# Decay of the state, x's remainder and the parts of the next q and k issued behind the last step of P's parts

## The chip, the cores and the metric

One NeuronCore of a Trainium2 chip runs the whole program. The metric is the device time of one execution in microseconds (us). "Profiled execution" is one further execution, recorded instruction by instruction; every duration below comes from it.

## The reference

Two stages follow each other. The first is an mLSTM recurrence over 768 steps for 4 batches and 8 heads with heads of 40 numbers; its output, one row of 320 numbers for each of 3072 tokens, is the `x` of the second, a bilinear feed-forward block with 1536 hidden units. All inputs are float32.

```python
for t in range(S):                                   # batch b, head h
    m_new  = maximum(f_gate[t] + m, i_gate[t])
    f_stab = exp(f_gate[t] + m - m_new);  i_stab = exp(i_gate[t] - m_new);  m = m_new
    C = f_stab * C + i_stab * outer(v[t], k[t])
    n = f_stab * n + i_stab * k[t]
    y[t] = sigmoid(o_gate[t]) * (C @ q[t]) / maximum(abs(n . q[t]), 1)
...
out = ((x @ w_a) * (x @ w_b)) @ w_out                # x: 3072 x 320, d_ff 1536
```

## The kernel before

The recurrence is computed in chunks of 128 steps of one batch: 24 chunks, numbered `n`, four batches to a time step of 128. The feed-forward block (the code calls it `moe_block`) takes the tokens of 2 or 3 chunks at a time: nine blocks of 2, 2, 3, 3, 3, 3, 3, 2, 3 chunks, with 12 hidden tiles each (`up` makes a hidden tile, `down` adds its product with w_out). While TensorE works on block `k`, the chunks of block `k`+2 go through the recurrence; the chunks' pieces are dealt out between the block's matmuls by a ratio written in the main loop.

A chunk from number 6 on goes through these stages; chunks 0 to 5 take a shorter road (`begin_*`).

- `stage_a`: q and k are each split into three bfloat16 parts h, m and l. ScalarE (ACT) copies h (L508), VectorE (DVE) subtracts it, giving the remainder `r` (L512), ACT copies m from r (L513), and DVE, for chunks below 8 GpSimd (POOL), subtracts again to get l (L515). ACT lays the parts out once more (L518, L519), and SyncE's queue (SP) issues four DMA transposes into the tiles `T` (L522): two for q, two for k. `T` has one buffer for each of q and k.
- `stage_e`: the decay matrix `E`, tile `gbc`: a DMA from DRAM (L224, issued on SP), a mask on POOL (L483), and eight exponentials on ACT (L490). `gbc` has two buffers.
- `stage_b`, once for each half of the heads: TensorE (PE) makes the scores `pS` from `T` (L545), DVE multiplies them with E (L550), and the product P is split into three bfloat16 parts: ACT takes the first (L552), DVE subtracts it (L554), and a last DVE step makes the third (L556). The parts lie in `pb` and in the upper halves of `gbc`.
- `stage_i`: PE multiplies q's parts with the state (L571), DVE scales the result (L575).
- `stage_c`: PE multiplies P's parts with v's parts into `pV` (L603), the first four heads with the parts of half 0, the last four with those of half 1; DVE adds (L610).
- `stage_u`: PE makes the update of the state in `pU` (L628); DVE decays the state `cst` (L635) and adds the update (L639); ACT, POOL and DVE split the state, and DMAs bring the parts into place for the chunk four later (L646 to L659).
- `stage_f`: normaliser and output gate (L669 to L686). `stage_d`, for chunk n-1: PE transposes the output into `pX` (L707), ACT copies it into `xh` (L711), and DVE makes the remainder `xl` (L712). xh and xl are the feed-forward block's inputs.

`pS`, `pI`, `pX`, `pV` and `pU` take turns in two PSUM banks (tag `pat`), so each must wait until the one two places earlier has been read. The feed-forward products `pu` have three banks.

The order on each engine is not the order of the code: a scheduler, with a model of its own for the durations, orders all instructions of an engine by what is ready when. Each engine then runs its list strictly in order, and waits where the next entry is not ready. `tc.issue_after(x)` tells the scheduler that instructions traced in its block stand behind instruction `x` on that engine; it adds no wait on the chip, only a place in the list. In the code, the stages of a step come as B, D, E, A, C, U, F: chunk n's P, chunk n-1's x, chunk n+1's E and q/k parts, then chunk n's products, update and output.

Of the kernel before, what the change touches and what calls it, by code (L numbers as in the profile page):

```python
# [8 lines left out]
F32 = mybir.dt.float32  # L9
# [6 lines left out]
ALU = mybir.AluOpType  # L16
# [4 lines left out]
def kernel(  # L21
# [13 lines left out]
    nc = tc.nc  # L35
    B, H, S, D = q.shape
    DM, DFF = w_a.shape
    P = 128
# [3 lines left out]
    DV = D + 2  # L42
# [38 lines left out]
    HH = H // 2  # L81
# [10 lines left out]
    for j in range(3):  # L92
        r = slice(j * BH, (j + 1) * BH)
# [18 lines left out]
    dec = wpool.tile([P, NC - 2, BH // 2], F32, name="dec")  # L112
# [12 lines left out]
    after = {}  # L125
# [53 lines left out]
    def nat(n):  # L179
        return inner.get(n) or (qk[n % NQ], va[n % NQ])  # L180
# [146 lines left out]
    def beta_col(c, b):  # L327
        return g_col(c, b, 0)
# [35 lines left out]
    def need(x):  # L364

        while ready[0] < x:
            next(conv)
# [104 lines left out]
    def half(h):  # L472

        return h % 2 * 64, h % 2 * HH + h // 2, h // 2

    st = {}

    def stage_e(n):

        c, b = chunks[n]  # L480
        E = gbc.pop(n)
        st.setdefault(n, {})["E"] = E
        nc.gpsimd.affine_select(  # L483
            E, E, pattern=[[0, H], [1, P]], compare_op=ALU.is_ge, fill=-1e30, base=0,
            channel_multiplier=-1,
        )
        yield
        beta = beta_col(c, b)
        for h in range(H):
            nc.scalar.activation(E[:, h], E[:, h], AF.Exp, bias=beta[:, h:h + 1])  # L490
            if h % 2 == 1:
                yield

    def stage_a(n):

        c, b = chunks[n]
        s = st.setdefault(n, {})
        src = [x[..., 0:D] for x in nat(n)[0]]
        need(32)
        for _ in conv:  # L500
            pass

        at = {"h": (0, 2 * D), "m": (D, D), "l": (2 * D, 0)}
        s["T"] = []
        for j in range(2):
            qks = qks2[j]
            ph, pm, pl = (qks[:, 1, :, at[i][j]:at[i][j] + D] for i in "hml")
            nc.scalar.copy(ph, src[j])  # L508
            yield
            r = apool.tile([P, H * DV], F32, tag="tmp", name=f"r{n}_{j}")[:, 0:H * D]  # L510
            r = r.rearrange("t (h d) -> t h d", h=H)
            (nc.gpsimd if 2 * n + j < 4 else nc.vector).tensor_tensor(r, src[j], ph, op=ALU.subtract)  # L512
            nc.scalar.copy(pm, r)  # L513
            yield
            (nc.gpsimd if n < 8 else nc.vector).tensor_tensor(pl, r, pm, op=ALU.subtract)  # L515
            yield
            lo = (1 - j) * D
            nc.scalar.copy(qks[:, 0, :, lo:lo + 2 * D], qks[:, 1, :, D - lo:3 * D - lo])  # L518
            nc.scalar.copy(qks[:, 0, :, 2 * D * j:2 * D * j + D], ph)  # L519
            T = apool.tile([P, 2, H, P], BF16, tag=f"T{j}", name=f"T{n}_{j}", bufs=1)  # L520
            for w in range(2):
                nc.sync.dma_start_transpose(T[:, w], qks[:, w].rearrange("t h d -> t (h d)"))  # L522
            s["T"].append(T)
            yield
# [12 lines left out]
    def stage_b(n, hf):  # L537
        s = st[n]
        qT, kT = s["T"]
        pS = ps_at.tile([P, HH, P], F32, tag="pat", name=f"pS{n}_{hf}")  # L540
        K3 = 3 * D
        for x in range(HH):
            h = hf * HH + x
            for w in range(2):
                nc.tensor.matmul(  # L545
                    pS[:, x, :], kT[0:K3, w, h, :], qT[0:K3, w, h, :], start=(w == 0), stop=(w == 1)
                )
        yield
        E = s["E"][:, hf * HH:(hf + 1) * HH]
        nc.vector.tensor_tensor(E, pS, E, op=ALU.mult)  # L550
        pb = apool.tile([P, 2, HH, P], BF16, tag="pb", name=f"pb{n}_{hf}")
        nc.scalar.copy(pb[:, 0], E)  # L552
        yield
        nc.vector.tensor_tensor(E, E, pb[:, 0], op=ALU.subtract)  # L554
        mid = E.bitcast(BF16).rearrange("s h (t w) -> s h t w", w=2)[:, :, :, 1]
        nc.vector.tensor_tensor(pb[:, 1], E, mid, op=ALU.subtract)  # L556
        s[f"pb{hf}"] = (pb[:, 0], mid, pb[:, 1])
        yield

# [55 lines left out]
    def stage_u(n):  # L615
        c, b = chunks[n]
        if c == NC - 1:
            return
        vw = vws.pop(n)
        if NS <= n < 6:  # L620
            pU = ps_dn.tile([P, 512], F32, tag="pd2", name=f"pU{n}")
        else:
            pU = ps_at.tile([P, 512], F32, tag="pat", name=f"pU{n}")
        pu = pU[:, 0:HH * DV].rearrange("p (h d) -> p h d", h=HH)
        dense(n, pU, 3)
        for h in (*range(0, H, 2), *range(1, H, 2)):
            r, _, x = half(h)
            nc.tensor.matmul(  # L628
                pu[r:r + 64, x], nat(n)[0][1][:, h, :], vw[:, h], start=True, stop=True
            )  # L630
        t = cst[b]
        if c == 0:
            nc.scalar.copy(t, pu)
        else:
            nc.vector.tensor_tensor(  # L635
                t, t, dec[:, c - 1, b * HH:(b + 1) * HH].unsqueeze(2).broadcast_to([P, HH, DV]),
                op=ALU.mult,
            )
            nc.vector.tensor_tensor(t, pu, t, op=ALU.add)  # L639
        yield  # L640
        if n + B < NF32:
            return
        cb = apool.tile([P, 3, HH, DV], BF16, tag="cb", name=f"cb{n}", bufs=1)
        cr = apool.tile([P, H * DV], F32, tag="tmp", name=f"cr{n}")[:, 0:HH * DV]
        cr = cr.rearrange("t (h d) -> t h d", h=HH)
        nc.scalar.copy(cb[:, 2], t)  # L646
        nc.gpsimd.tensor_tensor(cr, t, cb[:, 2], op=ALU.subtract)
        yield
        if n < 8:
            nc.scalar.copy(cb[:, 1], cr)  # L650
        else:
            nc.vector.tensor_copy(cb[:, 1], cr)
        nc.gpsimd.tensor_tensor(cb[:, 0], cr, cb[:, 1], op=ALU.subtract)
        for j in range(2):
            cd = c_dram[b][:, :, j * HH:(j + 1) * HH].rearrange("i d h e -> d i h e")
            nc.sync.dma_start(cd[:, 3], cb[j * 64:j * 64 + D, 2])
            nc.sync.dma_start(cd[:, 0:3], cb[j * 64:j * 64 + D])
        for w in range(2):
            nc.sync.dma_start(  # L659
                cx[b][w], c_dram[b][w:w + 3].rearrange("i d h e -> (i d) h e")  # L660
            )
        yield
# [30 lines left out]
    def stage_d(n):  # L693
# [10 lines left out]
        xh, xl = xt[k_]  # L704
        pX = ps_at.tile([P, 512], F32, tag="pat", name=f"pX{n}")
        for t in range(3):
            nc.tensor.transpose(pX[:, t * P:(t + 1) * P], s["y"][:, t * P:(t + 1) * P], ident)  # L707
        yield
        px = pX[:, 0:3 * P].rearrange("p (a t) -> p a t", a=3)
        cols = slice(t0, t0 + P)  # L710
        after["a"] = [nc.scalar.copy(xh[:, :, cols], px).ins]  # L711
        nc.vector.tensor_tensor(  # L712
            xl[:, :, cols], px, xh[:, :, cols].bitcast(F32), op=ALU.subtract
        )
        yield ("done", n)


# [353 lines left out]
    for kb in range(NB):  # L1071
# [5 lines left out]
        for x, _ in enumerate(moe_block(kb)):  # L1077
# [3 lines left out]
            while acc >= 1.0 and not done:  # L1081
                acc -= 1.0
                r = next(att, ("done", 99))
                done = r is not None and r[1] >= last
        while not done:
            r = next(att, ("done", 99))
# [31 lines left out]
```

## Time and profile before

| | |
|---|---|
| median of 3 runs (lowest, highest) | 563.04 us (562.67 to 563.28) |
| the profiled execution's own time | 560.51 us |
| its span, first to last instruction | 558.5 us |
| busy: PE, weight loads, DVE, ACT, POOL | 544.9, 518.0, 389.4, 267.9, 126.9 us |
| granted TensorE clock, mean | 0.993 |

The profiled execution's time has 2.0 us beside the span, and it is 2.5 us under the median of the other runs. In the rows further down, "x" after a group is the number of instructions, a duration is that of one instruction or of a merged run, and what stands in brackets is how long the engine sat idle before it and which instruction released it.

### The profile page before, as it was taken

How to read it: one execution, taken by the hardware profiler on the slowest of the kernel's cores; microseconds unless marked ns; L12 is line 12 of the kernel's file. 1: busy time of each engine (PE TensorE's matmuls, PEld its weight loads, DVE VectorE, ACT ScalarE, POOL GpSimd, SP SyncE). 2: the span in 40 equal slices, each digit the busy share in tenths (PEclk: the TensorE clock that was granted, in tenths of full speed). 3: DMA queues.
4: the chain of work that ended last, by engine and by line, in shares of the span. 5: the costliest groups of instructions: out<-in, count | busy, mean ns of one | idle time of the engine just before them, and what ended most of it. 6: DMA issues, size and time to landing. Idle time of an engine off the chain costs nothing.

```text
span 558.5 us, 12726 instructions
## 1 busy us (share of the span) xinstructions
PE 544.9 (98%) x4925; PEld 518.0 (93%) x4925; DVE 389.4 (70%) x888; ACT 267.9 (48%) x645; POOL 126.9 (23%) x188
## 2 busy tenths in 40 slices
PE   8999999899999999999999999999999999999997
PEld 6898898799999899999989999998999999999997
DVE  6889999964858683968749774977757755944332
ACT  5574678752626761556525654644526733310111
POOL 3102414641232320332031330333021302000000
PEclk9799999999999999999999999999999999999999
DMA  9999941393649762569536684586539704200001
GB/s 191 215 263 291 290 72 51 94 179 71 108 103 193 141 139 58 123 142 180 107 99 156 108 151 115 118 145 138 118 97 154 144 0 115 48 1 25 0 1 35
DMA packets 198551, 66.75 MB, mean 120 GB/s; under 512 B 184220, under 2 KB 191772, under 8 KB 198492
## 3 DMA queue, kind: packets, MB, share of 16 engines
q1 hardware_dynamic: 198444, 65.86, 56.4%
q8 instruction: 38, 0.62, 0.5%
q14 instruction: 21, 0.17, 0.1%
q10 hardware_dynamic: 48, 0.10, 0.0%
HBM read 41.11 MB, written 5.95 MB: 84 GB/s over the span
## 4 chain that ended last, share of the span: by engine, by line
PE 60%; DMA 17%; DVE 10%; ACT 5%; issue 3%; SPq 3%; POOL 1%; ACTq 0%; DVEq 0%; POOLq 0%
PE pu L810 31%; PE pd L781 15%; DMA T<-qks 4%; DMA c_dram<-cb 3%; ACT gbc L490 3%; DMA va<-in_v_dram 2%; PE pV L603 2%; PE pU L628 2%; DVE gbc L554 2%; DMA gbc<-g_dram 1%; DMA raw<-in_moe_w_a_dram 1%; DVE pb L556 1%; PE pS L884 1%; PE pV L927 1%; PE pS L545 1%
## 5 line engine op out<-in xcount | busy, mean ns | idle before, releaser
L810 PE MATMUL pu<-xh,w 128*128 128x384 f32 (+1 forms) x1080 | 276.5, 324 | 2.6 <-ACT g L816 0.9
L810 PE MATMUL pu<-xl,w 128*128 128x384 f32 (+1 forms) x648 | 208.0, 322 | 0.0
L810 PEld LDWEIGHTS pu<-xh,w 128*128 128x128 f32 x1080 | 190.6, 189 | 5.9 <-ACT g L816 1.3
L781 PE MATMUL pd<-w,gh 128*128 128x320 f32 x576 | 126.7, 309 | 0.0
L810 PEld LDWEIGHTS pu<-xl,w 128*128 128x128 f32 x648 | 122.2, 189 | 0.2
L817 DVE TENSOR_TENSOR g<-pu,g 128x384 f32<-128x384 f32 (+1 forms) x108 | 54.6, 505 | 89.4 <-PE pu L810 46.3
L781 PEld LDWEIGHTS pd<-w,gh 128*128 128x128 f32 x576 | 96.7, 188 | 0.1
L781 PE MATMUL pd<-w,gl 128*128 128x320 f32 x288 | 85.3, 310 | 0.0
L816 ACT COPY g<-pu 128x384 f32<-128x384 f32 (+1 forms) x90 | 39.6, 440 | 93.4 <-PE pu L810 84.2
L490 ACT ACTIVATE gbc<-gbc,gtab 128x128 f32<-128x128 f32 x160 | 49.1, 389 | 18.1 <-POOL gbc L483 18.0
L821 DVE TENSOR_TENSOR gl<-g,gh 128x384 fp32r<-128x384 f32 (+1 forms) x92 | 52.2, 568 | 1.9
L781 PEld LDWEIGHTS pd<-w,gl 128*128 128x128 f32 x288 | 53.1, 188 | 0.2
L585 POOL TENSOR_TENSOR vw<-va,gtab 128x336 f32<-128x336 f32 x20 | 16.4, 822 | 160.3 <-PE pU L628 135.2
L819 DVE CAST gh<-g 128x384 fp32r<-128x384 f32 (+1 forms) x108 | 41.1, 382 | 2.2
L483 POOL TENSOR_SCALAR_AFFINE_SELECT gbc<-gbc 128x1024 f32<-128x1024 f32 x20 | 22.6, 1132 | 65.1 <-DMA gbc<-g_dram 32.9
L554 DVE TENSOR_TENSOR gbc<-gbc,pb 128x512 f32<-128x512 f32 x36 | 27.2, 757 | 6.8 <-ACT pb L552 6.6
L603 PEld LDWEIGHTS <-pb 128*128 128x128 bf16 x576 | 23.4, 96 | 6.4 <-DVE pb L556 3.2
L684 POOL TENSOR_TENSOR osig<-osig,den 128x320 f32<-128x320 f32 x22 | 16.6, 754 | 54.9 <-DVE den L671 42.9
L603 PE MATMUL pV<-va,pb 128*128 128x42 bf16 x288 | 25.9, 183 | 2.7 <-DVE pb L556 2.7
L790 ACT COPY o<-pd 128x320 f32<-128x320 f32 x24 | 8.8, 434 | 40.3 <-PE pd L781 40.3
L550 DVE TENSOR_TENSOR gbc<-pS,gbc 128x512 f32<-128x512 f32 x36 | 23.7, 682 | 4.0 <-PE pS L545 4.0
L518 ACT COPY qks<-qks 128x640 bf16<-128x640 bf16 x36 | 26.0, 725 | 0.6
(154 smaller groups left out, 849.6 us busy)
## 6 DMA issues: line engine op xcount, KB each, us to landing
gbc<-g_dram SPq DMA_DIRECT2D x20, 512.0 KB
q<-in_q_dram SPq DMA_DIRECT2D x24, 160.0 KB
k<-in_k_dram SPq DMA_DIRECT2D x24, 160.0 KB
va<-in_v_dram SPq DMA_DIRECT2D x24, 160.0 KB
osig<-in_o_gate_dram SPq DMA_DIRECT2D x24, 160.0 KB
raw<-in_moe_w_out_dram SPq DMA_DIRECT2D x12, 320.0 KB
out_dram<-o SPq DMA_DIRECT2D x24, 160.0 KB
raw<-in_moe_w_a_dram SPq DMA_DIRECT2D x8, 384.0 KB
```

What stands on the lines that cost most here:

```text
L483: nc.gpsimd.affine_select(E, E, pattern=[[0, H], [1, P]], compare_op=ALU.is_ge, fill=-1e30, base=0, channel_multiplier=-1,)
L490: nc.scalar.activation(E[:, h], E[:, h], AF.Exp, bias=beta[:, h:h + 1])
L518: nc.scalar.copy(qks[:, 0, :, lo:lo + 2 * D], qks[:, 1, :, D - lo:3 * D - lo])
L550: nc.vector.tensor_tensor(E, pS, E, op=ALU.mult)
L554: nc.vector.tensor_tensor(E, E, pb[:, 0], op=ALU.subtract)
L603: nc.tensor.matmul(pv[:, h], pb[i][:, h % HH, :], vb[j][:, h], start=(x == 0), stop=(x == len(terms) - 1),)
L781: nc.tensor.matmul(pd[t][:, 0:DM], a[:, cols], w, start=(ff == 0 and first), stop=(ff == NF - 1 and last),)
L810: nc.tensor.matmul(acc[j], a, r, start=(x == 0), stop=(x == len(terms) - 1),)
L816: (nc.vector.tensor_copy if ff in [1, 2] else nc.scalar.copy)(g, acc[0])
L817: nc.vector.tensor_tensor(g, acc[1], g, op=ALU.mult)
L819: nc.vector.tensor_copy(gh, g)
L821: (nc.gpsimd if kb * 12 + ff < 16 else nc.vector).tensor_tensor(gl, g, gh.bitcast(F32), op=ALU.subtract)
```

## The change

Four kinds of DVE instructions are put behind the last step of the latest traced P (`after["b"]`: L556 of half 1, for chunk n since the stages that follow it in the code come after both halves): the decay of chunk n's state, `xl` of chunk n-1, and for q and k of chunk n+1 the remainder `r` and, from chunk 8 on, the part l. Nothing is added or taken away: each engine has the same instructions as before, in another order. (`r` had a branch for chunks below 2, which never come here.)

```diff
+    def parts():
+        return tc.issue_after(after["b"]) if "b" in after else nullcontext()
...
-            (nc.gpsimd if 2 * n + j < 4 else nc.vector).tensor_tensor(r, src[j], ph, op=ALU.subtract)
+            with parts():
+                nc.vector.tensor_tensor(r, src[j], ph, op=ALU.subtract)
...
-            (nc.gpsimd if n < 8 else nc.vector).tensor_tensor(pl, r, pm, op=ALU.subtract)
+            with parts() if n >= 8 else nullcontext():
+                (nc.gpsimd if n < 8 else nc.vector).tensor_tensor(pl, r, pm, op=ALU.subtract)
...
-        nc.vector.tensor_tensor(pb[:, 1], E, mid, op=ALU.subtract)
+        after["b"] = nc.vector.tensor_tensor(pb[:, 1], E, mid, op=ALU.subtract).ins
...
-            nc.vector.tensor_tensor(t, t, dec..., op=ALU.mult)
+            with parts():
+                nc.vector.tensor_tensor(t, t, dec..., op=ALU.mult)
...
-        nc.vector.tensor_tensor(xl[:, :, cols], px, xh..., op=ALU.subtract)
+        with parts():
+            nc.vector.tensor_tensor(xl[:, :, cols], px, xh..., op=ALU.subtract)
```

Since the scheduler orders everything anew, rows move on other engines too. Three places for chunks 12 and 13 stand for chunks 8 to 20. In the changed file line numbers are higher by 3 to 7 (L550 becomes L555, L556 L561, L512 L516, L515 L520, L635 L641, L712 L719, L522 L527).

DVE before, from just behind the score products of chunk 12 to the end of its P; r13_1 (L512) stands one row further up:

```order
L817 TENSOR_TENSOR g3_5_3884<-pu3_5_1_3802,g3_5_3884 128x384
L652 CAST cb10_3880<-cr10_3881 128x168
L635 TENSOR_TENSOR cst2_98<-cst2_98,dec_124 128x168
L554 TENSOR_TENSOR gbc12_3386<-gbc12_3386,pb12_0_3683 128x512
L575 TENSOR_TENSOR num12_3710<-pI12_3711,gtab_123 128x336
L819 CAST gh3_5_3927<-g3_5_3884 128x384
L554 TENSOR_TENSOR gbc12_3386<-gbc12_3386,pb12_1_3701 128x512
L556 TENSOR_TENSOR pb12_0_3683<-gbc12_3386 128x512
L515 TENSOR_TENSOR qks1_95<-r13_1_3788,qks1_95 128x8x40
L712 TENSOR_TENSOR xl4_3495<-pX11_3730,xh4_3494 128x3x128
L821 TENSOR_TENSOR gl3_5_3929<-g3_5_3884,gh3_5_3927 128x384
L556 TENSOR_TENSOR pb12_1_3701<-gbc12_3386 128x512
```

and in the changed kernel, from the same point:

```order
L559 TENSOR_TENSOR gbc12_3386<-gbc12_3386,pb12_0_3683 128x512
L559 TENSOR_TENSOR gbc12_3386<-gbc12_3386,pb12_1_3701 128x512
L561 TENSOR_TENSOR pb12_0_3683<-gbc12_3386 128x512
L824 TENSOR_TENSOR g3_6_3989<-pu3_6_1_3980,g3_6_3989 128x384
L580 TENSOR_TENSOR num12_3710<-pI12_3711,gtab_123 128x336
L561 TENSOR_TENSOR pb12_1_3701<-gbc12_3386 128x512
L516 TENSOR_TENSOR r13_0_3768<-q1_86,qks0_94 128x320
L516 TENSOR_TENSOR r13_1_3788<-k1_87,qks1_95 128x320
L641 TENSOR_TENSOR cst0_96<-cst0_96,dec_124 128x168
L719 TENSOR_TENSOR xl4_3495<-pX11_3730,xh4_3494 128x3x128
L826 CAST gh3_6_4000<-g3_6_3989 128x384
L520 TENSOR_TENSOR qks0_94<-r13_0_3768,qks0_94 128x8x40
```

P's steps now stand close together; both remainders of chunk 13, the decay and xl have moved behind them, and the l parts behind those.

SP before, the transposes of chunk 12 and the load of the next decay matrix (`gbc13`):

```order
L522 DMA_TRANSPOSE T12_0_3539<-qks0_94 128x8x128 x2
L522 DMA_TRANSPOSE T12_1_3556<-qks1_95 128x8x128 x2
L657 DMA c_dram1_127<-cb9_3639 40x3x168 x2
L186 DMA q1_86<-in_q_dram 128x8x40
L224 DMA gbc13_3625<-g_dram_125 128x1024
```

and in the changed kernel:

```order
L186 DMA q0_84<-in_q_dram 128x8x40
L527 DMA_TRANSPOSE T12_0_3539<-qks0_94 128x8x128 x2
L527 DMA_TRANSPOSE T12_1_3556<-qks1_95 128x8x128 x2
L224 DMA gbc13_3625<-g_dram_125 128x1024
L663 DMA c_dram1_127<-cb9_3639 40x3x168 x2
```

The load of gbc13 stands behind the four transposes in both, now directly.

PE before, the first scores of chunk 13 among the feed-forward products (`pu3_8_0` is hidden tile 8 of block 3):

```order
L810 MATMUL pu3_8_0_4047<-xh3_2541,w18_1136 128x384
L810 MATMUL pu3_8_0_4047<-xh3_2541,w20_1156 128x384
L545 LDWEIGHTS T13_1_3797
L545 MATMUL pS13_0_3909<-T13_0_3782,T13_1_3797 128x128
L545 LDWEIGHTS T13_1_3797
L545 MATMUL pS13_1_3932<-T13_0_3782,T13_1_3797 128x128
L810 MATMUL pu3_8_0_4047<-xl3_2542,w20_1156 128x384
```

and in the changed kernel:

```order
L817 MATMUL pu3_9_0_4081<-xl3_2542,w28_1352 128x384
L550 LDWEIGHTS T13_1_3797
L550 MATMUL pS13_0_3909<-T13_0_3782,T13_1_3797 128x128
L550 LDWEIGHTS T13_1_3797
L550 MATMUL pS13_1_3932<-T13_0_3782,T13_1_3797 128x128
L817 MATMUL pu3_9_1_4082<-xh3_2541,w25_1306 128x384
```

The scores of chunk 13 have moved back by one hidden tile. Counted in the same lists from the last matmul of `pV10` to the first of `pS13`, PE had 112 up and 54 down matmuls, and now has 129 and 63; to the first of `pS12` it had 64 and 27, and now has 73 and 30. The other matmuls of these stretches are the same.

More of the change, by code (lines that the diff above doesn't have):

```diff
@@ L634, in stage_u @@
         else:
[L635 to L638, printed above, removed]
+            with parts():
+                nc.vector.tensor_tensor(
+                    t, t, dec[:, c - 1, b * HH:(b + 1) * HH].unsqueeze(2).broadcast_to([P, HH, DV]),
+                    op=ALU.mult,
+                )
             nc.vector.tensor_tensor(t, pu, t, op=ALU.add)
@@ L711, in stage_d @@
         after["a"] = [nc.scalar.copy(xh[:, :, cols], px).ins]
-        nc.vector.tensor_tensor(
-            xl[:, :, cols], px, xh[:, :, cols].bitcast(F32), op=ALU.subtract
-        )
+        with parts():
+            nc.vector.tensor_tensor(
+                xl[:, :, cols], px, xh[:, :, cols].bitcast(F32), op=ALU.subtract
+            )
         yield ("done", n)
```

## The prediction

> **What bounds the kernel now.** I read the page first, then who waits for whom, the windows, and the timelines around chunks 9, 12, 13, 22 and 23.
>
> ```profile
> PE 544.9 (98%) x4925; PEld 518.0 (93%) x4925; DVE 389.4 (70%) x888; ACT 267.9 (48%) x645; POOL 126.9 (23%) x188
> ```
> ```profile
> 40.00:480.00 440.00, 432.59 (x4038) 412.81 (x4036) 323.46 (x734) 231.56 (x567) 118.83 (x154) 1.00 0.62 130
> ```
>
> PE is the bound: of a span of 558.5 us it is idle for 13.6, and for 7.4 (440 less 432.59) in the long middle where recurrence and feed-forward run together. Nothing is added to or taken from any engine, so the time can change only by what PE waits. The waits of the middle that concern this change are these (total us, times, longest):
>
> ```profile
> PE pV L603 <- DVE pb L556: 2.7, 5, 0.9
> PE pX L707 <- DVE gbc L550: 1.0, 2, 0.7
> ```
> ```profile
> DVE r L512 <- ACT qks L508: 31.5, 17, 3.6
> DVE gbc L554 <- ACT pb L552: 6.6, 5, 2.0
> PEld L603 <- DVE pb L556: 3.2, 5, 1.0
> PEld pX L707 <- DVE gbc L550: 1.2, 2, 0.8
> ```
>
> Five times PE waits for the third part of P, twice for a score product to be read out of its bank. The DVE rows say why: DVE stands 31.5 us in 17 waits before a remainder `r`, with P's steps queued behind. What else stands in front of P's last step shows in chunk 9 on DVE (start, duration), with the wait that it ends on PE:
>
> ```profile
> 186.29 0.32 DVE L635 TENSOR_TENSOR cst<-cst,dec 128x168 f32<-128x168 f32 x1
> 186.53 0.69 DVE L554 TENSOR_TENSOR gbc<-gbc,pb 128x512 f32<-128x512 f32 x1
> ...
> 187.40 0.69 DVE L554 TENSOR_TENSOR gbc<-gbc,pb 128x512 f32<-128x512 f32 x1
> 188.00 0.50 DVE L575 TENSOR_TENSOR num<-pI,gtab 128x336 f32<-128x336 f32 x1
> 188.42 0.68 DVE L556 TENSOR_TENSOR pb<-gbc 128x512 bf16<-128x512 f32 x1
> 189.02 0.48 DVE L515 TENSOR_TENSOR qks<-r,qks 128x320 bf16<-128x320 f32 x1
> 189.42 0.55 DVE L821 TENSOR_TENSOR gl<-g,gh 128x384 fp32r<-128x384 f32 x1
> 189.89 0.55 DVE L712 TENSOR_TENSOR xl<-pX,xh 128x384 fp32r<-128x384 f32 x1
> 190.36 0.68 DVE L556 TENSOR_TENSOR pb<-gbc 128x512 bf16<-128x512 f32 x1
> ```
> ```profile
> 190.05 0.18 PE L603 MATMUL pV<-vr,gbc 128*128 128x42 bf16 x1
> 191.10 0.22 PE L603 MATMUL pV<-va,pb 128*128 128x42 bf16 x2 [0.86 <-DVE pb L556]
> ```
>
> **What it gives back.** From start to start, the decay took 0.24 us, the l part 0.40 and xl 0.47: 1.1 us ahead of a step for which PE waited 0.86. The change moves all three behind it, and with them r, which is what kept L550 from the two `pX`. I therefore count all seven waits as gone. Their price is not the 3.7 us of the PE rows: there, idle time runs from the modelled end of the last matmul. In the rows above, PE issued nothing from 190.05 to 191.10, 1.05 us, where 0.86 is named. The weight loads' rows have 3.2 and 1.2, 4.4 us for the same waits, and 3.7 times 1.05/0.86 is 4.5. I take −4.4; the ends are −3.7 and −4.5.
>
> The Trainium skill (Perfetto Trace Analysis, Identifying the Most-Contended Engine) says that matmul busy time misleads on the room that is left, and that the share of LDWEIGHTS is to be read in its place. By matmul rows the sum below would end at 561.4, by weight-load rows at 560.7; the gap of 1.05 against 0.86 agrees with the page.
>
> **What it makes late.** No engine has more work, so the other costs are those of lateness: the decay, xl, r and l come after P. The decay is next needed by the addition behind `pU`, the xl by `pU`'s bank (it reads `pX`, whose bank `pU` takes) and by a feed-forward block a block later. Both stand within about 1.5 us behind P's last step (r, r, decay, xl: 0.4 + 0.4 + 0.24 + 0.47), while all of `pV`'s second half lies ahead of `pU` on PE; I cost them at nothing, and at up to 0.8 us a chunk where PE itself arrives late. The state's parts go to the chunk four later, also nothing. The q/k parts have no such cover: the transposes of chunk n+1 now start only after P of chunk n, and the scores of n+1 need them. P of chunk n in turn waits on ACT behind the exponentials of n+1, and these for a load that stands on SP behind the transposes of n. That is a ring, and the sum is how long one turn of it lasts against what PE has to do. Its rows, around chunks 11 and 12, with a slower sample of the same steps (load at 238.55, transposes at 184.83), the landing of a transpose (112.53, 115.34) and the one place where both r come back to back (446.82):
>
> ```profile
> 222.25 0.33 SPq L224 DMA_DIRECT2D gbc<-g_dram  x1
> ...
> 231.71 5.29 SPq L522 DMA_TRANSPOSE T<-qks  x4
> ...
> 238.55 0.53 SPq L224 DMA_DIRECT2D gbc<-g_dram  x1
> ```
> ```profile
> 226.12 1.23 POOL L483 TENSOR_SCALAR_AFFINE_SELECT gbc<-gbc 128x1024 f32<-128x1024 f32 x1 [0.52 <-DMA gbc<-g_dram]
> ...
> 243.88 1.09 POOL L483 TENSOR_SCALAR_AFFINE_SELECT gbc<-gbc 128x1024 f32<-128x1024 f32 x1 [2.71 <-DMA gbc<-g_dram]
> ```
> ```profile
> 227.38 2.46 ACT L490 ACTIVATE gbc<-gbc,gtab 128x128 f32<-128x128 f32 x8 [0.97 <-POOL gbc L483]
> ...
> 230.09 1.14 ACT L552 CAST pb<-gbc 128x512 bf16<-128x512 f32 x2
> ```
> ```profile
> 446.82 0.49 DVE L512 TENSOR_TENSOR r<-q,qks 128x320 f32<-128x320 f32 x1 [0.86 <-ACT qks L508]
> ```
> ```profile
> 448.11 1.35 ACT L518 COPY qks<-qks 128x640 bf16<-128x640 bf16 x2
> ```
> ```profile
> 184.83 6.53 SPq L522 DMA_TRANSPOSE T<-qks  x4
> ```
> ```profile
> 112.53 1.26 SPq L522 DMA_TRANSPOSE T<-qks  x1
> ...
> 115.34 0.84 PE L545 MATMUL pS<-T,T 120*128 120x128 bf16 x12 [0.40 <-DMA T<-qks]
> ```
>
> One turn, from the issue of the load: to the mask 3.9 (222.25 to 226.12) or 5.3 (238.55 to 243.88), taken as 4.3, since in the new list no q load goes just ahead; to the exponentials 1.3 (226.12 to 227.38); to L552 2.7 (227.38 to 230.09); L552 to the end of P 3.95 in the new order (0.57 for the first L552; 0.6 for each of two L554 and the first L556; 0.47 and 0.42 for g and num; 0.68 for the last L556); then two r and their copies until the first transpose, 2.0 (446.82 to half of the L518 pair, 448.8); four transposes 5.3 or 6.5, taken as 5.3. Sum: 19.6 us, with ends of 19.2 and 21.8. A transpose lands 1.55 us after its issue ended (113.79 to 115.34).
>
> PE's side, by the interval of an up matmul (175 ns), a down matmul (146 ns) and a narrow up matmul of the two-chunk blocks (120 ns):
>
> ```profile
> 206.11 2.80 PE pu L810 x16
> 208.91 1.31 PE pd L781 x9
> ...
> 131.42 0.96 PE pu L810 x8
> ```
> ```profile
> 242.41 0.79 PE L545 MATMUL pS<-T,T 120*128 120x128 bf16 x11
> ```
> ```profile
> 259.31 0.29 PE L545 MATMUL pS<-T,T 120*128 120x128 bf16 x2
> ```
>
> ```profile
> SPq L224 <- PE pV L603: 9.6, 2, 8.5
> ```
>
> At each third chunk SP's load waits until `pV` has freed the buffer; for gbc12 that was at 222.25, behind pV10. Call that 0. PE reached pS12 at 20.2 and pS13 at 37.1. The list now holds 9 up and 3 down matmuls more before pS12 (2.0 us) and 17 and 9 more before pS13 (4.3 us): 22.2 and 41.4, less 0.2 for a wait for P that goes. T12 lands at 19.6 + 1.55, 21.1: cover 1.1 us. T13 takes two turns and lands at 40.7: cover 0.5 us. So the third chunk of each three (10, 13, 16, 19) just gets by, and waits when a turn is over 19.8; each us above costs two there. With transposes of 6.5 in one turn of two the wait is 0.7, with 5.3 in both none; I charge 0.4 us to each, +1.6 for the four (ends 0, and 4 x 3.8 for a turn of 21.8). Chunk 23 has no such cover:
>
> ```profile
> 476.50 0.68 DVE L556 TENSOR_TENSOR pb<-gbc 128x512 bf16<-128x512 f32 x1
> ```
> ```profile
> 480.74 1.07 PE L545 MATMUL pS<-T,T 120*128 120x128 bf16 x16
> ```
>
> P22 ends at 477.2; 2.0, 5.3 and 1.55 later, at 486.0, T23 has landed. PE reached pS23 at 480.74 and has 29 narrow up and 9 down matmuls more in front of it now (4.8 us): 485.5. That is +0.5.
>
> **Sum.** −4.4 + 1.6 + 0.5 = −2.3. The profiled execution took 560.51 us, 2.5 under the median of the others; on the median of 563.04 it makes 560.7.
>
> **Rivals.** *The ring is too slow* (slower). A turn of 20.9, the load at 5.3 and transposes at 5.8, gives waits for T of 2.2 us at chunks 10, 13, 16 and 19 and 1.0 at 23: 9.8 − 4.4 = +5.4, 568.4 us. The gain is gone from a turn of 20.3 on. For it: both long samples occurred in the trace. Against: PE's scores have moved back by 4.3 us.
>
> *P still ends late* (no change). P's steps wait for ACT's L552, which stands behind the exponentials; DVE waited 6.6 us in five waits there. If half of the 4.4 stays, −2.2 + 2.1 leaves 562.9. Against: in chunk 9 DVE took 4.5 us from the first L554 to the end of P (186.53 to 191.04) and needs 3.4 by the new list.
>
> *Nothing new waits* (a larger gain): −4.5, 558.5.
>
> *The clock falls.* Between 20 and 40 us the granted clock was 0.86, a loss of 2.8 us in 20:
>
> ```profile
> 20.00:40.00 20.00, 19.96 (x178) 16.82 (x177) 16.61 (x42) 14.15 (x31) 2.04 (x3) 0.86 1.17 238
> ```
>
> Were a wait for T to bring that on, a turn of 21.4 (3.2 us of wait, four times, 1.5 at chunk 23) with four such falls would give 563.0 − 4.4 + 12.8 + 1.5 + 11.2, about 584 us; the middle ran at 1.00 with waits of up to 0.9. The Trainium skill (TensorE: Matmul & The Clock Gate, Why this matters for your kernels) puts the bound at PE idle for more than about 3 us; no wait of the middle is that long, so no row bears it out.
>
> **How the numbers follow.** Forecast 0.37; nothing new waits 0.20; P still late 0.20; ring too slow 0.21; clock 0.02. 0.2% is 1.1 us, about what a measurement here can tell from no change. The forecast and the larger gain are faster: 0.57; same 0.20; slower 0.23. The range goes from just under the larger gain, 558.3, to halfway into the slow ring, 566.0; the likeliest case alone has 559.5 to 562.
>
> **What would show it.** Right: the row of pV waiting for pb and that of pX waiting for L550 vanish; L512's waits on DVE shrink and L554's for L552 grow; DVE's L556 follows L552's start by about 4 us; pS waits for T at chunk 23 by half a us, and by less than 1 at 10, 13, 16 and 19. Wrong: waits of pS for T of 2 us and more, or pV still waiting for pb, or new waits of pu for g because DVE stands before L554.

## The result, and the profile after

The changed kernel is slower: 576.7 us median of six runs (573.8 to 583.4) against 562.2 us of the kernel before (559.2 to 563.3); the ratio is 1.027, 95% interval 1.024 to 1.031. The slowest of the six, 583.4, fell into a second, slower state that some executions show; ratios and means, here and below, are without such executions. The profiled execution took 575.85 us, its span is 574.1 us, its mean granted clock 0.981 (before 0.993). Span times granted clock is an estimate of what the span would have been at full clock. Its mean is 564.6 us for the changed kernel and 555.0 for the kernel before, and 9.2 and 4.0 us are lost to the clock: by that estimate about two thirds of the loss would be there at full clock too, and one third is clock.

In the changed kernel's file L817 is the up matmul, L823 ACT's copy `g` out of its bank, L824 the product, L797 and L798 the copy and the store of a block's output `o`, L652 and L662 to L665 the state's parts `cb` with their stores and loads, L527 the transposes. First, who waits for whom: PE's rows of the middle (112 to 480 us), ACT's and DVE's of the whole execution (total us, times, longest):

```profile
PE pu L817 <- ACT g L823: 7.2, 5, 2.2
PE pu L817 <- DVE g L824: 1.1, 2, 0.7
PE pS L550 <- DMA T<-qks: 0.6, 2, 0.4
...
ACT qks L511 <- DMA T<-qks: 43.5, 15, 5.2
DVE gbc L559 <- ACT pb L557: 36.4, 13, 5.3
ACT cb L652 <- DMA c_dram<-cb: 33.1, 12, 5.2
```

The rows of pV waiting for pb and of pX waiting for the score product are gone. In their place PE waits 7.2 us for `g`, at the first hidden tile of a block. ACT's rows say what is late: the transposes have not yet read `qks` when ACT wants to write q's next h part (43.5 us, before 19.9), and the store of `cb` has not gone (33.1 us, before 11.3).

Where it comes from shows on SP at the end of block 2 (start, duration), before:

```profile
202.02 5.30 SPq L522 DMA_TRANSPOSE T<-qks  x4
207.42 0.97 SPq L659 DMA_DIRECT2D cx<-c_dram  x2
208.44 0.70 SPq L656 DMA_DIRECT2D c_dram<-cb  x2
218.61 1.33 SPq L791 DMA_DIRECT2D out_dram<-o  x3
222.25 0.33 SPq L224 DMA_DIRECT2D gbc<-g_dram  x1
```

and after:

```profile
216.58 6.60 SPq L527 DMA_TRANSPOSE T<-qks  x4
223.27 0.86 SPq L663 DMA_DIRECT2D c_dram<-cb  x2
224.22 2.35 SPq L798 DMA_DIRECT2D out_dram<-o  x3
226.68 0.86 SPq L665 DMA_DIRECT2D cx<-c_dram  x2
227.59 0.70 SPq L662 DMA_DIRECT2D c_dram<-cb  x2
228.33 0.34 SPq L224 DMA_DIRECT2D gbc<-g_dram  x1
```

Before, the transposes of chunk 11 ended 15 us ahead of the load of gbc12, which went as soon as pV10 had freed the buffer. Now they end at 223.2, and the block end's stores and loads stand behind them without a gap: the load starts at 228.33, 3.5 us behind the start of pV10's last matmul (224.81), where before it was 0.19. At the ends of blocks 3, 4 and 5 it is 2.6, 2.3 and 3.0 us late, against 0.19 before at each.

ACT and PE at the same place (in brackets the wait and what ended it), and PE's same wait at the ends of blocks 4 and 5:

```profile
222.40 0.46 ACT L511 CAST qks<-q 128x320 bf16<-128x320 f32 x1 [4.84 <-DMA T<-qks]
...
225.56 0.33 ACT L652 CAST cb<-cst 128x168 bf16<-128x168 f32 x1 [1.55 <-DMA c_dram<-cb]
225.79 0.42 ACT L797 COPY o<-pd 128x320 f32<-128x320 f32 x1
226.14 0.48 ACT L823 COPY g<-pu 128x384 f32<-128x384 f32 x1
```
```profile
226.67 0.44 PE L817 MATMUL pu<-xh,w 128*128 128x384 f32 x1 [1.42 <-ACT g L823]
...
357.29 0.44 PE L817 MATMUL pu<-xh,w 128*128 128x384 f32 x1 [1.70 <-ACT g L823]
...
423.39 0.69 PE L817 MATMUL pu<-xh,w 128*128 128x384 f32 x1 [2.21 <-ACT g L823]
```

Two entries that wait for SP stand ahead of `g` on ACT; before, ACT's list had nothing between the block's three `o` and this `g`. The granted clock fell at such waits (windows of the changed kernel: busy time of PE and of the other engines, clock, DMA share, GB/s), and the long middle as a whole ran fewer matmuls, the kernel before first and the changed one second:

```profile
220.00:240.00 20.00, 18.58 (x175) 17.61 (x174) 11.66 (x26) 7.94 (x22) 4.33 (x5) 0.91 0.52 127
340.00:360.00 20.00, 18.30 (x168) 16.98 (x167) 10.76 (x24) 11.44 (x25) 3.23 (x5) 0.95 0.69 152
420.00:440.00 20.00, 17.79 (x186) 16.28 (x183) 14.24 (x32) 8.42 (x22) 4.06 (x5) 0.83 0.43 98
```
```profile
112.00:480.00 368.00, 362.74 (x3494) 349.83 (x3494) 253.87 (x563) 183.47 (x444) 90.44 (x117) 1.00 0.61 123
```
```profile
112.00:480.00 368.00, 358.78 (x3309) 343.76 (x3308) 236.71 (x533) 176.95 (x428) 93.12 (x115) 0.98 0.58 118
```

### The profile page after: what moved, and what is told of

It reads as the page before. It is cut to its first block, busy times and chain, and to the rows that moved or that the text cites. A ratio compares the mean times of both kernels' runs of the same rounds, so it can differ in the third digit from the quotient of the medians.

```text
span 574.1 us, 12712 instructions
## 1 busy us (share of the span) xinstructions
PE 553.4 (96%) x4925; PEld 523.6 (91%) x4925; DVE 383.3 (67%) x888; ACT 267.4 (47%) x645; POOL 130.9 (23%) x188
## 4 chain that ended last, share of the span: by engine, by line
PE 60%; DMA 10%; DVE 9%; issue 8%; SPq 6%; ACT 4%; POOL 3%; ACTq 0%; POOLq 0%; DVEq 0%
PE pu L817 33%; PE pd L788 14%; DMA va<-in_v_dram 4%; PE pV L608 2%; PE pU L633 2%; SPq L527 2%; DMA c_dram<-cb 2%; DMA osig<-in_o_gate_dram 2%; PE pS L550 2%; ACT gbc L493 1%; DMA out_dram<-o 1%; DVE g L824 1%; SPq L663 1%; DVE gl L828 1%; PE pS L891 1%
## 5 line engine op out<-in xcount | busy, mean ns | idle before, releaser
L817 PE MATMUL pu<-xh,w 128*128 128x384 f32 (+1 forms) x1080 | 280.8, 329 | 8.7 <-ACT g L823 7.2
L817 PE MATMUL pu<-xl,w 128*128 128x384 f32 (+1 forms) x648 | 209.7, 325 | 0.0
L817 PEld LDWEIGHTS pu<-xh,w 128*128 128x128 f32 x1080 | 194.1, 193 | 12.6 <-ACT g L823 9.2
L817 PEld LDWEIGHTS pu<-xl,w 128*128 128x128 f32 x648 | 124.7, 193 | 0.1
L824 DVE TENSOR_TENSOR g<-pu,g 128x384 f32<-128x384 f32 (+1 forms) x108 | 54.8, 508 | 102.4 <-PE pu L817 56.6
L823 ACT COPY g<-pu 128x384 f32<-128x384 f32 (+1 forms) x90 | 39.6, 441 | 86.7 <-PE pu L817 81.1
L559 DVE TENSOR_TENSOR gbc<-gbc,pb 128x512 f32<-128x512 f32 x36 | 24.8, 714 | 36.5 <-ACT pb L557 36.4
L826 DVE CAST gh<-g 128x384 fp32r<-128x384 f32 (+1 forms) x108 | 39.8, 369 | 1.9
L653 POOL TENSOR_TENSOR cr<-cst,cb 128x168 f32<-128x168 f32 x18 | 14.1, 782 | 105.5 <-DVE qks L520 105.4
L555 DVE TENSOR_TENSOR gbc<-pS,gbc 128x512 f32<-128x512 f32 x36 | 23.7, 684 | 11.8 <-PE pS L550 11.4
L511 ACT CAST qks<-q 128x320 bf16<-128x320 f32 x18 | 8.3, 459 | 44.5 <-DMA T<-qks 40.1
L517 ACT CAST qks<-r 128x320 bf16<-128x320 f32 x36 | 15.6, 459 | 25.6 <-DVE r L516 25.6
```

The costliest lines, as they stand in the source:

```text
L817: nc.tensor.matmul(acc[j], a, r, start=(x == 0), stop=(x == len(terms) - 1),)
L823: (nc.vector.tensor_copy if ff in [1, 2] else nc.scalar.copy)(g, acc[0])
L824: nc.vector.tensor_tensor(g, acc[1], g, op=ALU.mult)
L826: nc.vector.tensor_copy(gh, g)
```

## The experiments

"Lists" are the orders of an engine's instructions. A turn is the time from one load of `gbc` to the next, a round is three turns, from one load that waits for pV at a block's end to the next. The expectations name theories. A: ACT reaches the first `g` copy of a block too late, and PE waits for it; A2: the store of `o` is what holds g's buffer. B: the loss is early, up to 112 us. C: whatever is done on ACT, what is late makes PE wait at another place. R: late transposes hold up all that stands behind them on SP; R2: above all the load at a round's end. Q: what counts is that T is late and the turns are slow, not SP's queue.

The table has, for each kernel, the median of all its runs, the ratio to the kernel before in runs beside it, the span at full clock and the clock loss (means; the kernel before had 554.1 to 555.7 and 3.5 to 4.4 in the runs beside these), the time from gbc12's load to gbc14's, two turns of the ring, and how late the load at a round's end is: from the start of pV's last matmul, at chunks 10, 13, 16 and 19. Rows and the last two columns come from the one profiled execution of each kernel, which can lie away from the median: e6's took 565.2 us, e13's 567.8, e14's 570.6.

| | us | ratio, 95% interval | full clock, loss | two turns | load late |
|---|---|---|---|---|---|
| before | 562.2 | | 555.0, 4.0 | 34.7 | 0.19 |
| changed | 576.7 | 1.027 (1.024–1.031) | 564.6, 9.2 | 39.6 | 2.3–3.5 |
| e1 | 572.0 | 1.018 (1.013–1.023) | 561.3, 9.1 | 39.3 | 2.0–3.2 |
| e2 | 571.5 | 1.021 (1.014–1.027) | 563.1, 7.0 | 39.4 | 2.0–3.9 |
| e3 | 571.4 | 1.019 (1.015–1.024) | 563.1, 6.1 | 38.9 | 1.4–3.8 |
| e4 | 558.9 | 0.996 (0.993–1.000) | 554.3, 2.8 | 34.6 | 0.19 |
| e5 | 572.5 | 1.017 (1.008–1.027) | 562.4, 5.7 | 39.2 | 1.8–3.9 |
| e6 | 571.8 | 1.021 (1.014–1.029) | 560.9, 6.8 | 39.2 | 0.9–3.1 |
| e7 | 559.7 | 0.999 (0.995–1.003) | 554.9, 3.1 | 35.1 | 0.19 |
| e8 | 575.1 | 1.026 (1.018–1.034) | 565.4, 7.3 | 39.3 | 2.3–4.1 |
| e9 | 584.9 | 1.042 (1.035–1.048) | 571.3, 10.9 | 38.2 | 0.46–2.5 |
| e10 | 571.2 | 1.017 (1.012–1.022) | 562.7, 6.4 | 31.5 | 0.46 |
| e11 | 561.5 | 1.000 (0.997–1.003) | 553.7, 5.3 | 31.4 | 0.19 |
| e12 | 560.8 | 0.999 (0.996–1.002) | 554.3, 4.3 | 34.2 | 0.19 |
| e13 | 561.7 | 1.006 (1.002–1.010) | 556.9, 4.2 | 40.4 | 0.19 |
| e14 | 565.0 | 1.012 (1.003–1.021) | 557.5, 6.4 | 38.8 | 0.19 |
| e15 | 559.4 | 0.999 (0.995–1.002) | 553.6, 3.7 | 34.4 | 0.19 |
| e16 | 575.5 | 1.028 (1.022–1.035) | 563.8, 9.0 | 40.0 | 2.1–3.9 |
| e17 | 562.8 | 1.003 (1.000–1.005) | 556.8, 3.4 | 38.7 | 0.19 |

**Which of the moved instructions.** e4 and e12 are one kernel: `r` and `l` free, decay and `xl` behind P.

```diff
-            with parts():
+            with nullcontext():
                 nc.vector.tensor_tensor(r, src[j], ph, op=ALU.subtract)
...
-            with parts() if n >= 8 else nullcontext():
+            with nullcontext():
```

> Only the decay and xl behind P; r and l where the scheduler puts them. ACT's list has nothing between the block's last outputs and the first g copy; the early list is that of the changed kernel up to about 100 us. Theory A: no waits of pu for g of over 1 us at the block ends, no half-clock stretch there: 562 to 567, by how much of the early loss (6.8) stays. Theory C for decay and xl (late, they hold pU's bank or the addition): 568 or more, with PE waiting for cst or xl.

> The kernel of e4 again (only the decay and xl behind P), in more rounds: e4 had a ratio of 0.9964 to the kernel before, with an interval just over 1 at the end. If the two waits of pX and some of pV's five are its gain, it comes out at 0.994 to 0.998 here; if e4 was chance, at 1.000.

Decay and `xl` cost nothing and bring nothing that 22 runs can tell: 0.996 and 0.999, both intervals holding 1. Theory C for them is refuted. The reverse, `r` alone behind P, with `parts()` taken from decay, `xl` and `l`:

```diff
-            with parts() if n >= 8 else nullcontext():
+            with nullcontext():
...
-            with parts():
+            with nullcontext():
                 nc.vector.tensor_tensor(t, t, dec..., op=ALU.mult)
```

> Only r behind P (l needs r, so it stands behind P too); decay and xl where the scheduler puts them. Theory A2: ACT's list has the same entries ahead of g at the ends of blocks 2 to 5, SP's the same transposes ahead of the stores: 570 to 576, waits of pu for g of 5 us and more. A theory that decay and xl behind P cost something of their own, by holding pU's bank: 565 to 570 here.

1.026: the whole loss is that of `r` (and of `l`, which needs `r`). Then by k and q (e11 has j == 1, e16 has j == 0 in both places):

```diff
-            with parts():
+            with parts() if j == 1 else nullcontext():
                 nc.vector.tensor_tensor(r, src[j], ph, op=ALU.subtract)
...
-            with parts() if n >= 8 else nullcontext():
+            with parts() if n >= 8 and j == 1 else nullcontext():
```

> The change with r and l of k alone behind P; r and l of q stay where the scheduler puts them, so that q's two transposes can go before P ends and two instead of four are late. ACT's list has no q copy ahead of the first g copy at the blocks' ends. Theory R: under half of the loss stays, 559 to 566. Theory Q: T of k is as late as before, so 568 or more.

> The complement of e11: r and l of q alone behind P, those of k free. SP issues q's transposes first and k's behind them in the list, so all four are late again. Both theories: as the changed kernel, 570 to 577, the load 1.5 us or more behind pV. If it is under 565, it was the number of late r, not the late first transpose, that made the loss.

With k's alone the loss is gone (1.000). e16 came out as 1.028, but it is no separate case: on every engine its list is that of the changed kernel, instruction for instruction, so k's `r` and `l` stand behind P there even where they are free. It repeats the changed kernel and says nothing of q's `r` alone. In e11 two transposes go ahead of the end of P, at 205.52, and the load is on time:

```profile
205.52 2.60 SPq L527 DMA_TRANSPOSE T<-qks  x2
...
214.26 2.58 SPq L527 DMA_TRANSPOSE T<-qks  x2
...
223.47 1.34 SPq L798 DMA_DIRECT2D out_dram<-o  x3
227.10 0.33 SPq L224 DMA_DIRECT2D gbc<-g_dram  x1
```

**Early or late, and ACT's list.** e1 puts the first `g` copy ahead of the q and state copies at the ends of blocks 2 to 5, and leaves PE's, DVE's and POOL's lists as they are in the changed kernel. e2 lets the change begin with chunk 8's P; e3 does both.

```diff
+                    if ff == 0:
+                        after["g"] = gi          # gi: the g copy
...
+            with tc.issue_after(after["g"]) if j == 0 and n in (12, 15, 18, 21) else nullcontext():
                 nc.scalar.copy(ph, src[j])
...
+        with tc.issue_after(after["g"]) if n in (9, 12, 15, 18) else nullcontext():
             nc.scalar.copy(cb[:, 2], t)
```
```diff
-        return tc.issue_after(after["b"]) if "b" in after else nullcontext()
+        return tc.issue_after(after["b"]) if "b" in after and after["n"] >= 8 else nullcontext()
```

> The changed kernel with one thing put back: at the ends of blocks 2 to 5 ACT takes the first g copy of the next block (L823) before the q copy of chunk 12, 15, 18 or 21 (L511) and the state copy of chunk 9, 12, 15 or 18 (L652), as the kernel before does. The lists of PE, DVE and POOL are those of the changed kernel, row for row. Theory A (ACT stands at the block's end behind late transposes and stores, PE waits for g, and the clock falls behind the wait): the four waits of pu for g (1.42, 0.55, 1.70, 2.21, sum 5.9 us) go, and with them four stretches of 3.4 us at half clock (6.8 us lost): 576 - 12.7 = 563 us. Theory B (the loss is in the early part, up to 112 us, where the decay has moved): nothing changes, 574 to 577. Theory C (the transposes are late whatever ACT does, so the wait only moves to pS for T, or to P): 570 to 576, with waits of pS for T of 2 us and more.

> The change, but only from chunk 8's P on: the decay of chunks 6 and 7, xl of 5 to 7 and r and l of 7 and 8 keep their old places, so that the lists up to about 150 us are those of the kernel before; the ACT list at the ends of blocks 2 to 5 is as in the changed kernel. Theory A: the waits of pu for g and the half-clock stretches of the block ends stay; only what the early part lost goes, 3.4 us of waits and 3.4 us of clock: 569 us. Theory B (all of the loss is early): 560 to 563. Theory C: 572 to 576, as the ring turns the same from chunk 8 on.

> Both edits together: the change from chunk 8's P on, and the first g copy ahead of the q and state copies at the ends of blocks 2 to 5. Theories A and B together: the waits of pu for g go, the early loss goes, and what the change gave back (the waits of pV for P and of pX) stays: 556 to 560, faster than the kernel before. Theory C: 566 or more, with pS waiting for T.

All three stayed at 571 to 572 (ratios 1.018 to 1.021, at most a little under the changed kernel's 1.027), so A in this form and B both fall; C's times came true (e2's but for half a us), but in e1 PE waited only 1.7 us for T in the middle. In e1 the same wait of PE for `g` stood there, now because `g` itself waited: its buffer is one that `o` holds until its store has gone, and that store is behind the late transposes on SP.

```profile
417.22 1.08 ACT L802 COPY o<-pd 128x320 f32<-128x320 f32 x3 [3.64 <-PE pd L793]
423.62 0.48 ACT L828 COPY g<-pu 128x384 f32<-128x384 f32 x1 [5.31 <-DMA out_dram<-o]
```

B falls by e2, whose lists up to 125 us are those of the kernel before: it waited longer there than e1, which has the changed lists and no such row. The first row is e2's, the second that of e7, the kernel before but for its output stores:

```profile
PE pc L449 <- ACT g L824: 3.7, 1, 3.7
```
```profile
PE pc L449 <- ACT g L816: 1.9, 1, 1.9
```

So what differs up to 112 us in the two profiled executions, here and in the result, comes and goes from run to run.

**The output's stores.** e5 is the changed kernel with these stores issued by ACT, e6 the same on e1, e7 on the kernel before.

```diff
-                    nc.sync.dma_start(out[b * S + c * P:b * S + (c + 1) * P, :], o)
+                    nc.scalar.dma_start(out[b * S + c * P:b * S + (c + 1) * P, :], o)
```

> The changed kernel with the stores of the output issued by ACT, right behind its copies, instead of by SP, where they stand behind the late transposes. Theory A2 (the first g copy waits for a buffer that the output's tile o holds until its store has gone, and the store stands on SP behind the transposes): the part of the wait that L823 names, 1.64 to 1.72 us, goes; the entries ahead of it on ACT (L511 for the transposes, 4.7 to 4.8 us; L652 for c_dram's store, 1.3 to 1.9 us) stay and hold g up nearly as long: 568 to 574. Theory C (the wait moves to wherever PE next needs the late transposes): 570 to 576, with waits of pS for T.

> The first g copy ahead of the q and state copies on ACT at the ends of blocks 2 to 5 (as in e1) and the output's stores issued by ACT. Nothing late is now ahead of g: theory A2 has the waits of pu for g at the block ends (in e1 1.31, 1.88, 2.62 and 0.99, sum 6.8) gone, with the half-clock stretches behind them (two in e1, 3.4 us lost): 572 - 9 to 10 = 562 to 563. Theory C: still 568 or more, with waits of pS for T that add up to over 4 us.

> The kernel before with the output's stores issued by ACT. All theories: nothing late stands ahead of these stores there, so 559 to 562, within 0.4% of the kernel before; if it gains over 1%, e6's gain would be that of the stores' queue alone and says nothing on the change.

e7 is no change. e5 came out at 572.5, inside both ranges, with 6.5 us of waits for `g`, and tells nothing between A2 and C. In e6 the waits for `g` did go, 0.8 us instead of 7.2 in the profiled execution, and the kernel stayed 1.4 to 2.9% slower: A2 is right on the wait and wrong on its price. PE then waited elsewhere:

```profile
PE pX L718 <- DVE gbc L559: 2.0, 1, 2.0
PE pS L554 <- DMA T<-qks: 1.3, 4, 0.5
...
PE pu L822 <- ACT g L828: 0.8, 3, 0.3
```

**SP's queue.** e9 takes the loads of `gbc` and the stores of `cb` off SP, to POOL, and the output's stores to ACT; e10 does so in the kernel before.

```diff
-        return nc.sync.dma_start(t, g_dram[c - 1:c, ...
+        return nc.gpsimd.dma_start(t, g_dram[c - 1:c, ...
...
-            nc.sync.dma_start(cd[...
+            nc.gpsimd.dma_start(cd[...
```

> The changed kernel with what stands behind the transposes on SP taken off it: the loads of the decay matrix and the stores of the state's parts are issued by POOL, the output's stores by ACT; SP keeps the transposes, the loads of q, k, v and the gates, and of the state's parts. So far, with span x granted clock as the time at full speed: the kernel before has 554.5 us and loses 4.2 to the clock, the changed one 564.5 and 10.6. Theory R (r behind P makes the four transposes late; they hold up all that stands behind them on SP, and PE waits for whatever of it is next): full-speed part 555 to 558, clock loss 4 to 6, 561 to 565 us in all. Theory Q (what counts is only that T, and with it qks, is late, not SP's queue): full-speed part 561 or more, 568 or more in all, with waits of pS for T, or of pu for g behind L511.

> The kernel before with the same stores and loads off SP: what POOL's and ACT's issuing costs or brings by itself. 557 to 563 by both theories; it is the base for e9.

These two tell nothing between R and Q: e10, expected at 557 to 563, came out at 571.2 us, ratio 1.017 (1.012 to 1.022), so POOL's issuing costs by itself (the output's stores on ACT cost nothing in e7). Why is not known; the turns did not get longer by it (31.5 us for two). e9 had 584.9 us, 1.042 (1.035 to 1.048), and there the waits stood where the prediction had looked for them:

```profile
PE pS L550 <- DMA T<-qks: 12.8, 8, 4.9
```

e13 leaves SP its work and asks for one change in its list: on top of e6, the state's stores and loads stand behind the load of gbc12, 15, 18 and 21. The scheduler moved rows on the other engines too, but PE's first scores of chunk 13 have 128 up and 63 down matmuls ahead of them since pV10, in e6 131 and 63. e17 is e13 without `r` and `l` of chunks 21 to 23 behind P.

```diff
-                        load_g(n + 2)
+                        after["l"] = load_g(n + 2)
...
+        with tc.issue_after(after["l"]) if n in (8, 11, 14, 17) else nullcontext():
             for j in range(2):
                 ...
                 nc.sync.dma_start(cd[:, 3], cb[j * 64:j * 64 + D, 2])
```

> e6 with one thing more: at chunks 10, 13, 16 and 19 the state's stores and loads (L663, L665) stand on SP behind the load of the decay matrix two chunks later, so that this load follows the transposes directly. So far that load started 0.19 us behind the end of pV in every kernel that was not slower, and 1.4 to 4.1 us behind it in the slow ones. Theory R2 (four late transposes leave SP no time for the block end's DMAs ahead of this load; the late load then delays the whole next round of three chunks): the load is 0.2 us behind pV, 559 to 564 us. Theory Q (the two turns of the ring inside a round are too slow by themselves: 38 to 41 us now, 33 to 36 before): 567 or more, with a ratio as e6's 1.013 to 1.029.

> e13 without r and l of chunks 21 to 23, the last ones, behind P: there the rounds of three chunks are over, and blocks 6 to 8 of e13's profiled execution took 152.0 us (409.0 to 561.0) where those of the kernel before took 149.3. If the late r of the last chunks is what is left of the loss (e13 1.0058), blocks 6 to 8 take 149 to 150 and the ratio is 0.996 to 1.001; if it is something else of e13, the ratio stays at 1.003 to 1.008.

```profile
220.38 7.08 SPq L534 DMA_TRANSPOSE T<-qks  x4
228.78 0.35 SPq L224 DMA_DIRECT2D gbc<-g_dram  x1
229.19 0.36 SPq L671 DMA_DIRECT2D c_dram<-cb  x1
```

This is e13: the transposes end at 227.5, the load goes at pV's end, and the ratio falls from e6's 1.021 (1.014 to 1.029) to 1.006 (1.002 to 1.010), though two turns still take 40.4 us. R2 is right on this place. e17 comes to 1.003, its blocks 6 to 8 take 150.1 us (e13 152.0, before 149.3); that lies between the two values expected, so that what remains is not settled.

e14 and e15 split the change by chunks: `r` and `l` of 11, 14, 17 and 20 free, or these alone behind P (the line of `l` has the same condition).

```diff
-            with parts():
+            with parts() if n not in (11, 14, 17, 20) else nullcontext():   # e15: n in
                 nc.vector.tensor_tensor(r, src[j], ph, op=ALU.subtract)
```

> The change without r and l of chunks 11, 14, 17 and 20, whose transposes stand on SP just ahead of the block end's stores and the load; the other chunks' r and l, the decay and xl stay behind P. Theory R2: SP is free at the block's end, the load 0.2 us behind pV, 559 to 565. Theory Q: the two turns inside a round are as slow as in the changed kernel, 38 to 41 us; 567 or more.

> The other half: only r and l of chunks 11, 14, 17 and 20 behind P (with decay and xl); r and l of the others where the scheduler puts them. Theory R2: much of the loss stays, the load 1.5 to 3 us behind pV, 565 to 573. Theory Q: the turns inside a round are as before, 33 to 36 us, 558 to 563.

In e14 the load is on time and the median is at the top of R2's range (565.0; ratio 1.012, 1.003 to 1.021); e15 came out as Q had it (0.999) and against R2. But Q's reason is not borne out: e14's and e13's turns are as slow as the changed kernel's, and their rounds of three chunks, from one load at a block's end to the next, take no longer than before. In e14 the loads went at 232.09 and 294.23, 62.1 us apart; before, 62.8. Its block-end rows, with the load on time, and e15's:

```profile
228.74 1.33 SPq L798 DMA_DIRECT2D out_dram<-o  x3
232.09 0.33 SPq L224 DMA_DIRECT2D gbc<-g_dram  x1
```
```profile
205.67 5.29 SPq L527 DMA_TRANSPOSE T<-qks  x4
...
221.21 0.33 SPq L224 DMA_DIRECT2D gbc<-g_dram  x1
```

In e15 the first two turns of a round are short (34.4 us), so the third chunk's transposes, though behind P, end 10 us ahead of the load. What fits is the round as a whole: two turns, a third lap from the last load to the end of its transposes, and the block end's DMAs on SP. In the changed kernel, from gbc12's load at 228.33 on:

```profile
248.08 0.53 SPq L224 DMA_DIRECT2D gbc<-g_dram  x1
...
267.90 0.53 SPq L224 DMA_DIRECT2D gbc<-g_dram  x1
...
282.86 5.33 SPq L527 DMA_TRANSPOSE T<-qks  x4
...
293.81 0.35 SPq L224 DMA_DIRECT2D gbc<-g_dram  x1
```

The means of three rounds are 2 x 20.0 + 19.6 + 5.5 = 65.1 us. These are the pieces that the rounds of 65.5, 63.7 and 66.0 consist of, so the sum is no test; what says something is that the same rounds took 62.0 to 63.7 wherever the load waits only for pV, in the kernel before, in e13 and in e14. Take out the 5.5 (e13) or shorten the third lap (e14) or the first two (e15, e11), and the round fits. That reading was put together after the runs; no run was made to test it alone, and what is left of the loss in e14 (1.2%) and e13 (0.6%) is not explained by it.

## Why the prediction was wrong

The forecast was 560.7 us, with a range of 558.3 to 566.0; the kernel takes 576.7, above the range and slower instead of faster. The first score products of chunks 12 and 13 on PE in the changed kernel, whose loads of gbc12, 13 and 14 started at 228.33, 248.08 and 267.90:

```profile
250.39 0.29 PE L550 MATMUL pS<-T,T 120*128 120x128 bf16 x2
...
269.07 0.29 PE L550 MATMUL pS<-T,T 120*128 120x128 bf16 x2
```

By the steps of the prediction:

- **The seven waits go: right; what they are worth was not measured by itself.** Both rows vanish. The nearest measure is e11, where the round fits and no matmul of pV waits for pb: 553.7 us at full clock against 555.7 of the kernel before beside it, −2.0 (give or take 1.2, two standard errors) where −4.4 was charged. The clock loss was 1.8 higher (5.3 against 3.5), so that nothing is seen in the time. But other rows moved in e11 as well: in its profiled execution PE waited 1.4 us for `g` in the middle.
- **Decay and xl at nothing: right** (e4, e12).
- **One turn of the ring, 19.6 us: right** (mean of six 20.0, from 18.9 to 20.7), term by term too: the turn from gbc12's load had 4.1, 1.1, 2.7, 3.6, 2.0 and 6.3 us where 4.3, 1.3, 2.7, 3.95, 2.0 and 5.3 were added up. PE's arrival was right where the load is on time: in e13 and e14 the scores of the next two chunks came 21.9 to 22.9 and 40.7 to 41.7 us behind the load, foreseen at 22.2 and 41.4. In the changed kernel pS12 came at 22.1 (250.39 − 228.33) and pS13 at 40.7 (269.07), which agrees partly by luck: the load was 3.5 us late, and PE had lost about as much, 1.4 us to its wait for `g` and 1.7 to the clock; counted from pV10's end it came at 25.6. With the load and PE late alike, there remained the small waits of pS for T, 0.6 us in all in the middle (at chunks 10 and 15) and 0.1 at chunk 23, foreseen as 0.4 at each third chunk and 0.5 at chunk 23. The growth of DVE's wait for ACT's first part of P, from 6.6 to 36.4 us, came as foreseen.
- **The step that failed: "Call that 0".** The round was begun at pV's end, as if the load of each third chunk went on time whatever SP had in front of it (in the kernel before it does, 0.19 us behind pV at all four, though the row shown with that step names only two waits for pV), and its turns were counted up to the third chunk's scores, not to the next round's load. The third lap was left out: its transposes, of chunk 11, moved from 202.0 to 216.6, and the five us of block-end DMAs that stand behind them on SP. With the prediction's 3 x 19.6 and these five us it would have been 64 us against the 62.8 of this round before. Only the middle load, which stands directly behind the transposes, had been looked at. Of the 15.6 us between the two profiled spans, 8.5 were lost in the four rounds from gbc9's load to gbc21's, with their clock; 3.3 lie ahead of them, where profiled executions of one and the same list (e4 and e12) also differ by 2.6, and 3.8 behind, where the half clock from 422.7 to 429.6 us alone cost about 3.
- **Lateness was priced only where T is read.** Late transposes also keep `qks` from being written again (ACT's L511) and the queue from everything behind them. That is where most of PE's 7.2 us came from; "new waits of pu for g" was named, but by way of DVE, and it was ACT and SP.
- **The clock rival's condition was wrong.** It was tied to waits of 3.2 us and given 0.02. The clock fell at waits of 1.42, 1.70 and 2.21 us. "The time can change only by what PE waits" left the clock out, and about a third of the loss is clock.
- **Which rival came nearest:** "the ring is too slow" had the right direction and looked at the right chain, but its condition, a turn of over 20.3, was not what happened, PE's wait stood at another place, and its +5.4 us is little more than a third of the loss. (Its own inputs, the load at 5.3 and transposes at 5.8, make a turn of 21.1, not 20.9, and about 570 us.)

## What to carry to other kernels

When work on a queue is made later, follow that queue to the next point where it has to be empty, here the load at the end of a three-chunk round, and sum the whole round, not one turn; an engine's list and a DMA queue hold up everything behind a late entry, whatever it is for. A wait removed from PE without shortening what sets the round returns at another place: e6 took 6.4 us of waits for `g` away and did not get under 1.4% of loss, while on top of it four loads moved ahead of the state's stores and loads on SP (e13) brought most of it back. If the three DVE steps are wanted behind P, let q's part go first (e11): half of the transposes then have left before P ends.

## What was not expected of the hardware

The clock fell at short waits. Between 112 and 480 us the granted clock goes to half in stretches of 3.4 us, one or two in a row. The first of the changed kernel, behind its wait of 1.42 us, and the 3.4 us after it (behind the window's length stand PE's busy time and, in brackets, its matmuls; 0.50 and 1.00 are the granted clock):

```profile
228.20:231.60 3.40, 3.40 (x11) 3.40 (x12) 2.70 (x9) 0.24 (x1) 1.47 (x2) 0.50 0.74 198
231.60:235.00 3.40, 3.40 (x32) 3.30 (x32) 2.62 (x4) 1.43 (x5) 2.47 (x3) 1.00 0.53 92
```

Of the 43 waits of PE of 0.9 us and more between 112 and 480 us of all profiled executions, such a stretch came with 1 of the 19 of up to 1.38 us, 2 of the 6 from 1.42 to 1.54, and 17 of the 18 from 1.70 up (the exception is one of 2.36 us in e9); it began within 1.6 us of the wait's end, or inside the wait. The Trainium skill (TensorE: Matmul & The Clock Gate, Why this matters for your kernels) puts the bound at idle gaps of more than about 3 us. Here 14 of these 17 waits were shorter than that, from 1.70 us up, and the measurement decides; whether anything besides the wait's length plays a part is not shown. Three of the changed kernel's waits at the block ends (1.42, 1.70 and 2.21 us) came with four such stretches: 6.8 us of clock beside 5.3 us of wait.
